# Attention and a capacity-routed mixture of experts: the planner knows when a load's room is free, and phase 1's routing starts two remainders later

## The chip, the core and the metric

The kernel runs on one core of a Trainium2 chip. Each core has five engines with their own instruction queues: TensorE (PE: matrix products, with a weight load ahead of each matmul, shown as PEld), VectorE (DVE), ScalarE (ACT), GpSimd (POOL) and SyncE (SP). ACT, DVE and POOL run their instructions in the order in which they are written. Transfers are issued from SP and POOL queues and carried out by 16 DMA engines that all queues share. The metric is the time of one execution in microseconds of the device.

## The reference

```python
def _attn_ref(q, k, v):                      # q, k, v: 8 x 8 x 576 x 64
    scores = scale * np.matmul(q, k.transpose(0, 1, 3, 2))
    mask = (rel >= 0) & (rel < window)       # window 64
    ...
    return np.matmul(attn, v)

def _moe_ref(x, w_gate, w1, w2):             # x: 4608 x 512, 8 experts
    logits = x @ w_gate
    order = np.argsort(-logits.flatten())
    for idx in order:
        tok, e = (int(idx) // E, int(idx) % E)
        if assigned[tok] >= 0 or counts[e] >= cap:      # cap = 576
            continue
        assigned[tok] = e
        counts[e] += 1
    for e in range(E):
        mask = assigned == e
        h = np.maximum(x[mask] @ w1[e], 0.0)            # 512 -> 1024
        out[mask] = h @ w2[e]                           # 1024 -> 512
```

Attention with a sliding window of 64 gives 4608 tokens of 512 values. The tokens are given to experts greedily, the highest logit first, 576 to each expert. Each token then goes through the two layers of its expert.

## The kernel before

The first part (`attention`) computes the attention for all tokens and stores them to a tensor in memory. The second part has eight phases, one for each expert. In phase p the routing (`Routing.steps(p)`) finds which expert fills up next, and which tokens it gets: it computes each free token's best choice on DVE (`choices`, lines 448 to 455), finds the threshold in eight rounds of comparing on DVE (line 463) and counting on TensorE (lines 522 and 536), and makes a list of the expert's 576 tokens. The rounds need each other's results, so the routing of a phase is one long chain of small steps; the routing of phase p + 1 begins where that of phase p ends.

From the routing of a phase two streams start. `Experts.load(p)` brings the expert's weights: eight chunks of 512 KB (four of w1, four of w2) go from memory to six staging buffers `st` (line 789, issued from SP, but from POOL for the last four of phase 0). ACT rounds a chunk to `wh` (line 810), writes its negative to `wl` (line 819), and an accumulating DMA from POOL adds `st` to it (line 821), so that `wh` and `wl` together are the full weight. The first three chunks of phase 0 take a subtraction on DVE in place of it (line 814). A ring of eight pairs `wh`, `wl` holds one expert's weights; a chunk of the next phase enters when one is given back (line 805). A staging buffer comes free when its add has landed; with six buffers, chunk i needs the buffer of the chunk six before it.

`Experts.turn(p)` gathers the tokens with five indirect DMAs from POOL (line 862), transposes them on TensorE (line 875, two PSUM buffers `tp`), rounds them to `xh` on ACT (line 852) and takes the remainder `xl` on DVE (line 856), in tiles of 128 tokens. `Experts.steps(p)` does the products: sixteen units of the first layer, each twelve matmuls of 128 rows of h by 256 or 320 tokens (line 921: `wh xh`, `wl xh`, `wh xl`), with three PSUM rooms `h`. A unit is read by ACT (`hh`, line 893) and then by DVE (`hl`, line 898), which frees its room. The second layer (lines 953 and 963) follows, with its results scattered to the output by indirect DMAs from POOL (line 943).

The order of all this on each engine is written out in advance by a planner (`Streams`): a small event clock in nanoseconds, in which every stream (routing, loads, gathers, products, evacuations) is a generator. A generator that yields a number goes on after that time; one that yields a function goes on when the function is true. An instruction is put on its engine's queue at the moment at which its generator reaches it. The planner's clock has prices for matmuls and rough ones for DVE, POOL and the DMAs; the engines then wait for the real data. So a wrong price never makes a wrong result, but an instruction may stand too early in an engine's queue and hold up what is behind it.

In `load`, `there[i]` is the time at which the planner takes chunk i to have landed. Before ACT's instruction for the chunk is put down, the planner waits for the ring, and then for that time:

```python
t = max(self.clock(), there.get(i - 1, 0)) + (LOAD if p else 1500) * (1 if i else 2)
...
yield lambda: self.taken - self.ring < self.used
if there[i] > self.clock():
    yield there[i] - self.clock()
```

The constants are LOAD = 2600 and ADDED = 4500. `self.lows[p]` counts the tiles of phase p whose remainder (line 856) has been put down.

Of the kernel before, what the change touches and what calls it, by code (L numbers as in the profile page):

```python
# [281 lines left out]
def consts(tc, cp):  # L282
    nc = tc.nc
    c = dict(pool=cp, zero=cp.tile([128, 128], BF, name="zero"))

    c["jp"] = cp.tile([128, 128], I32, name="jp")
    c["rel"] = cp.tile([128, 128], I32, name="rel")
    nc.gpsimd.iota(c["jp"], pattern=[[1, 128]], base=0, channel_multiplier=-1)
    return c
# [58 lines left out]
class Routing:  # L348


    def __init__(self, ctx, tc, c, V):
        self.tc, self.nc, self.c, self.V = tc, tc.nc, c, V
        nc = tc.nc
        rt = ctx.enter_context(tc.tile_pool(name="rt", bufs=1))
        self.rt, self.ctx = rt, ctx

        def t(name, shape, dt=FT):
            x = rt.tile(shape, dt, name=name)
            setattr(self, name, x)
            return x  # L360

        for name in ("eid", "un", "m", "best"):
            t(name, [128, NJ])
        for name in ("oh", "w", "one"):
            t(name, [128, NJ, E], BF)
        t("G0", [128, NJ, ND], BF)
        t("cw", [128, E])
        t("dg", [128, ND], I32)
        t("lane", [128, 1])
        t("rows", [128, 1], U32)  # L370
        self.setup = self.constants(c["jp"], t)
        self.idx, self.eint = {}, {}
# [364 lines left out]
NCH = 4  # L737
# [3 lines left out]
STAGE = 6  # L741
# [3 lines left out]
LOAD = 2600  # L745
ADDED = 4500
# [3 lines left out]
class Experts:  # L750
    def __init__(self, ctx, tc, c, xs, w1, w2, out, ring=8):
        self.tc, self.nc, self.c = tc, tc.nc, c
        self.xs, self.w1, self.w2, self.out = xs, w1, w2, out
        self.ring = ring
        self.fw = ctx.enter_context(tc.tile_pool(name="fw", bufs=1))
        self.ps = ctx.enter_context(tc.tile_pool(name="fp", bufs=1, space=PSUM))
        self.W = {}
        self.XT = {}
        self.used = 0
        self.taken = 0  # L760
        self.first = 0
        self.gathered = 0
        self.sent = 0
        self.turned = 0
        self.tiles = [0] * E
        self.lows = [0] * E
# [10 lines left out]
    def load(self, p, ei):  # L777

        nc, fw = self.nc, self.fw
        yield lambda: self.taken == 2 * NCH * p  # L780
        e = nc.sync.value_load(ei[0:1, 0:1], min_val=0, max_val=E - 1)
        eg = nc.gpsimd.value_load(ei[0:1, 0:1], min_val=0, max_val=E - 1) if p == 0 else None
        st, there = {}, {}

        def fetch(i):
            st[i] = fw.tile([128, 1024], FT, name="st", bufs=STAGE)

            q, r = (nc.gpsimd, eg) if p == 0 and i >= 4 else (nc.sync, e)
            q.dma_start(st[i], self.part(i, r))

            t = max(self.clock(), there.get(i - 1, 0)) + (LOAD if p else 1500) * (1 if i else 2)
            if p == 0 and i == 4:

                t = max(t, self.clock() + self.busy(0, "pool") + FIRST)
            there[i] = t

        ahead = 3 if p else 4
        for i in range(ahead):
            fetch(i)
        if p == 0:  # L800
            yield lambda: self.gathered
        for i in range(2 * NCH):
            if p == 0 and i == 3:
                yield lambda: self.tiles[0] > 1
# [3 lines that stand above are left out]
            hi = fw.tile([128, 1024], FR, name="wh", bufs=self.ring)  # L808
            lo = fw.tile([128, 1024], FR, name="wl", bufs=self.ring)
            nc.scalar.activation(hi, st[i], AF.Copy)  # L810
            yield 1050
            yield lambda: self.gathered > p
            if self.quick(p, i):
                nc.vector.tensor_tensor(lo, st[i], hi.bitcast(FT), OP.subtract)
                self.W[p, i] = (hi, lo)
                dt = self.busy(1130, "dve")
            else:

                nc.scalar.activation(lo, hi.bitcast(FT), AF.Copy, scale=-1.0)  # L819
                yield 1150  # L820
                nc.gpsimd.dma_start(lo.bitcast(FT), st[i], accum_op=OP.add)  # L821
                self.spawn(self.ready(p, i, hi, lo), self.busy(650, "pool") + ADDED - 1200)
                dt = 1300
            self.taken += 1
            if i + ahead < 2 * NCH:
                fetch(i + ahead)
            yield max(100, dt - 1200) if p or i < 3 else 900
# [178 lines left out]
def body(tc, q, k, v, vt, wg, w1, w2, xs, out):  # L1006
    nc = tc.nc
    with ExitStack() as ctx:
        cp = ctx.enter_context(tc.tile_pool(name="cp", bufs=1))
        ctx.enter_context(tc.manual_schedule())  # L1010
        c = consts(tc, cp)
        wgs = cp.tile([128, HP, 32], FT, name="wgs")
        L = cp.tile([128, NJ, E], FT, name="L")
        rt = Routing(ctx, tc, c, L)
        with ExitStack() as actx:
            attention(actx, tc, c, q, k, v, vt, (wgs, wg), xs, L, lambda j0, j1: rt.choices(j0, j1, 0), rt.setup,
                      rt.counters)
        rt.start()
        ex = Experts(ctx, tc, c, xs, w1, w2, out)
        rt.spare = ex.room  # L1020

        st = Streams()
        ex.spawn, ex.busy, rt.busy, ex.clock = st.add, st.busy, st.busy, lambda: st.now
        ex.warm, ex.rows, rt.prime = rt.warm, rt.rows, ex.prime

        def route():
            for p in range(E):
                for dt in rt.steps(p):
                    if p in rt.eint and p not in known:
                        known.add(p)  # L1030
                        st.add(ex.load(p, rt.eint[p]))
                    if p in rt.idx and p not in listed:
                        listed.add(p)
                        st.add(ex.turn(p, rt.idx[p]))
                    yield dt

        def products():
            for p in range(E):
                yield lambda: p in ex.XT
                yield from ex.steps(p, rt.idx[p])  # L1040

        known, listed = set(), set()
        st.add(route())
        st.add(products())
        st.run()
# [17 lines left out]
```

## Time and profile before

| | |
|---|---|
| median of three runs | 671.07 us (670.53 to 671.51) |
| the profiled execution | 669.82 us, span 668.1 us |
| mean granted TensorE clock | 0.980 |
| TensorE busy | 636.8 us, 95% of the span |
| VectorE, ScalarE, GpSimd busy | 443.7, 361.7, 186.5 us |
| moved by DMA | 134.10 MB, mean 201 GB/s |

The span runs from the first to the last instruction. Attention takes it up to about 165 us; then comes the routing of phase 0, in which TensorE has little to do, and from 200 us to the end the products of the eight phases. In the timeline's rows the first number is the start in microseconds from the span's start, the second the length; then come the engine, the line, the operation, and what is written from what. A number in square brackets is the idle time of the engine just before, and what ended it. A row with xN is N instructions in a row.

### The profile page before, as it was taken

Reading aid. Unit: us, or ns where it says so; the run is one execution under the profiler, and the core shown is the slowest. Engines: PE = TensorE matmul, PEld = TensorE weight load, DVE = VectorE, ACT = ScalarE, POOL = GpSimd, SP = SyncE. Lnnn points to the kernel's source line nnn. Section 1 sums busy time; section 2 is a strip of 40 time slices with the busy share of each in tenths; the row PEclk is TensorE's granted clock in tenths of the full one; section 3 lists DMA queues with packets and bytes.
Section 4 is the critical chain, followed back from the end, with each engine's and each line's share of the span. In section 5 each row is a group of like instructions: output and inputs, shape, how many; then the busy total and the mean of one; then the engine's idle time right before and its main releaser. Section 6 shows DMA issues by size and latency. Waiting matters only on the chain. (4 is left out here: it accounts for less than half of the span.)

```text
span 668.1 us, 16948 instructions
## 1 busy us (share of the span) xinstructions
PE 636.8 (95%) x6383; PEld 535.1 (80%) x6383; DVE 443.7 (66%) x2246; ACT 361.7 (54%) x733; POOL 186.5 (28%) x218
## 2 busy tenths in 40 slices
PE   8999999997479999999999999999999999999995
PEld 6667777776459878987997898799889879879984
DVE  5878898888787776875796787688578742221300
ACT  5788988885056156427626543662744366534310
POOL 0433233330061033206304231530512155212111
PEclk9999999999579999999999999999999999999999
DMA  9999988922069169729757956965987598983401
GB/s 301 352 374 373 368 321 313 380 74 81 3 216 233 33 241 241 164 87 273 194 97 267 221 123 181 246 165 100 289 196 154 184 226 249 231 230 83 91 25 47
DMA packets 50097, 134.10 MB, mean 201 GB/s; under 512 B 4696, under 2 KB 10968, under 8 KB 50016
## 3 DMA queue, kind: packets, MB, share of 16 engines
q0 software_dynamic: 15280, 52.98, 35.3%
q1 hardware_dynamic: 34192, 79.52, 33.5%
q8 instruction: 50, 0.82, 0.5%
q10 hardware_dynamic: 544, 0.52, 0.2%
q14 instruction: 31, 0.25, 0.1%
HBM read 82.15 MB, written 18.87 MB: 151 GB/s over the span
## 5 line engine op out<-in xcount | busy, mean ns | idle before, releaser
L943 POOL DMA_INDIRECT out<-ot,idx x40 | 41.9, 1047 | 271.0 <-DVE ot L941 79.2
L893 ACT ACTIVATE hh<-h 128x256 fp32r<-128x256 f32 (+1 forms) x128 | 52.0, 408 | 99.2 <-PE h L921 98.1
L898 DVE SCALAR_TENSOR_TENSOR hl<-h,hh 128x256 fp32r<-128x256 f32 x128 | 53.3, 417 | 77.0 <-ACT hh L893 76.1
L963 PE MATMUL o<-wh,hh 128*128 128x512 f32 x256 | 102.5, 401 | 0.0
L963 PE MATMUL o<-wl,hh 128*128 128x512 f32 x256 | 101.8, 398 | 0.0
L963 PE MATMUL o<-wh,hl 128*128 128x512 f32 x256 | 101.5, 396 | 0.0
L135 DVE CUSTOM_DVE_ANT_0 st<-Sp,mask 128x128 f32<-128x128 f32 x288 | 78.9, 278 | 21.4 <-PE Sp L126 15.1
L145 ACT ACTIVATE pe<-st,mx 128x128 f32<-128x128 f32 x288 | 91.2, 391 | 3.3 <-DVE mx L135 3.3
L921 PE MATMUL h<-xh,wl 128*128 128x256 f32 (+1 forms) x512 | 93.0, 299 | 0.0
L921 PE MATMUL h<-xl,wh 128*128 128x256 f32 (+1 forms) x512 | 92.1, 298 | 0.6 <-DVE xl L856 0.6
L921 PE MATMUL h<-xh,wh 128*128 128x256 f32 (+1 forms) x512 | 91.9, 299 | 0.7 <-ACT xh L852 0.7
L921 PEld LDWEIGHTS h<-xh,wh 128*128 128x128 f32 x512 | 75.9, 189 | 1.5 <-ACT xh L852 0.8
L921 PEld LDWEIGHTS h<-xl,wh 128*128 128x128 f32 x512 | 75.7, 190 | 0.9 <-DVE xl L856 0.9
L921 PEld LDWEIGHTS h<-xh,wl 128*128 128x128 f32 x512 | 76.1, 190 | 0.2
L810 ACT ACTIVATE wh<-st 128x1024 fp32r<-128x1024 f32 x64 | 67.2, 1050 | 10.4 <-DMA st<-w 10.4
L821 POOL DMA_DIRECT2D wl<-st x61 | 56.5, 1245 | 35.7 <-ACT wl L819 33.4
L819 ACT ACTIVATE wl<-wh 128x1024 fp32r<-128x1024 f32 x61 | 64.4, 1056 | 0.8
L935 ACT ACTIVATE ot<-o 128x512 f32<-128x512 f32 x32 | 19.1, 598 | 81.6 <-PE o L963 80.1
L963 PEld LDWEIGHTS o<-wh,hl 128*128 128x128 f32 x256 | 48.1, 188 | 9.4 <-issue 0.4
L963 PEld LDWEIGHTS o<-wh,hh 128*128 128x128 f32 x256 | 48.2, 188 | 8.9
L963 PEld LDWEIGHTS o<-wl,hh 128*128 128x128 f32 x256 | 48.2, 188 | 8.6
L862 POOL DMA_INDIRECT xg<-xs,idx x40 | 40.9, 1024 | 45.5 <-DVE eq L706 35.1
(177 smaller groups left out, 1134.9 us busy)
## 6 DMA issues: line engine op xcount, KB each, us to landing
wl<-st POOLq DMA_DIRECT2D x61, 512.0 KB, 8.2
st<-w SPq DMA_DIRECT2D x60, 512.0 KB, 7.5
xs<-x SPq DMA_DIRECT2D x36, 256.0 KB, 4.9
VO<-v SPq DMA_DIRECT2D x6, 1168.0 KB, 17.0
VT<-vt SPq DMA_DIRECT2D x6, 1152.0 KB, 11.5
Q<-q SPq DMA_DIRECT2D x6, 1152.0 KB, 14.2
K<-k SPq DMA_DIRECT2D x6, 1152.0 KB, 15.7
VO<-v SPq DMA_DIRECT2D x4, 584.0 KB, 11.3
```

The lines of the kernel that those rows point to most:

```text
L135: nc.vector.tensor_tensor_reduce(st[:, h, :], Sp[h % 2][:, h // 2], mk, scale=-0.125, scalar=3.0e38, op0=OP.add, op1=OP.min, accum_out=mx[ ...
L145: nc.scalar.activation(pe[:, h, :], st[:, h, :], AF.Exp, bias=mx[:, h:h + 1], scale=-1.0)
L810: nc.scalar.activation(hi, st[i], AF.Copy)
L819: nc.scalar.activation(lo, hi.bitcast(FT), AF.Copy, scale=-1.0)
L821: nc.gpsimd.dma_start(lo.bitcast(FT), st[i], accum_op=OP.add)
L862: nc.gpsimd.indirect_dma_start(out=g[0:n, a], out_offset=None, in_=self.xs, in_offset=IndirectOffsetOnAxis(ap=idx[0:n, a:a + 1], axis=0))
L893: nc.scalar.activation(hh[:, f, c0:c1], h, AF.Relu)
L898: nc.vector.scalar_tensor_tensor(t, h[:, a - c0:b - c0], 0.0, hh[:, f, a:b].bitcast(FT), op0=OP.max, op1=OP.subtract)
L921: nc.tensor.matmul(h, wv[:, cc, 128 * (f % 2):128 * (f % 2) + 128], xt[:, cc, c0:c1], start=(k == 0), stop=(k == 11))
L935: nc.scalar.activation(ot, o, AF.Copy)
L943: nc.gpsimd.indirect_dma_start(out=self.out, out_offset=IndirectOffsetOnAxis(ap=idx[0:m, a:a + 1], axis=0), in_=ot[0:m], in_offset=None)
L963: nc.tensor.matmul(o, ht[:, f, 128 * a:128 * a + 128], wt[:, 512 * (f % 2):512 * (f % 2) + 512], start=(k == 0), stop=(k == 23))
```

## The change

There are two edits. The first: when a chunk's add is put down, the planner notes the time at which it reckons the add to have landed, plus 1000, in a new table `added`, under the chunk's number counted over all phases. A load's `there` then counts from the latest of the clock, the load before, and the note of the chunk six before, whose staging buffer it takes. The second: the routing generator of phase 1 first yields a function that is true once the remainders of two tiles of phase 0 have been put down.

```diff
@@ class Experts, __init__
         self.W = {}
+        self.added = {}
@@ load, fetch(i)
-            t = max(self.clock(), there.get(i - 1, 0)) + (LOAD if p else 1500) * (1 if i else 2)
+
+            t = max(self.clock(), there.get(i - 1, 0), self.added.get(2 * NCH * p + i - STAGE, 0))
+            t += (LOAD if p else 1500) * (1 if i else 2)
@@ load
                 nc.gpsimd.dma_start(lo.bitcast(FT), st[i], accum_op=OP.add)
-                self.spawn(self.ready(p, i, hi, lo), self.busy(650, "pool") + ADDED - 1200)
+                t = self.busy(650, "pool") + ADDED - 1200
+                self.spawn(self.ready(p, i, hi, lo), t)
+                self.added[2 * NCH * p + i] = self.clock() + t + 1000
@@ route
             for p in range(E):
+                if p == 1:
+                    yield lambda: ex.lows[0] > 1
                 for dt in rt.steps(p):
```

No instruction of an engine is added or taken away; the edits act on the order in which the planner writes them.

## The prediction

> **What bounds the kernel now.** I read the page first, then TensorE's idle time by stretches, then who it waited for, then the timeline at each place where it waits.
>
> ```profile
> span 668.1 us, 16948 instructions
> ...
> L898 DVE SCALAR_TENSOR_TENSOR hl<-h,hh 128x256 fp32r<-128x256 f32 x128 | 53.3, 417 | 77.0 <-ACT hh L893 76.1
> ...
> 168.00:185.00 17.00, 7.78 (x225) 6.54 (x224) 12.52 (x68) 0.00 (x0) 1.07 (x1) 0.50 0.01 3
> 185.00:200.00 15.00, 11.22 (x97) 8.99 (x98) 12.51 (x31) 8.19 (x11) 9.60 (x10) 0.81 0.76 236
> 200.00:656.00 456.00, 453.27 (x3178) 399.11 (x3178) 279.52 (x1107) 219.50 (x345) 129.96 (x135) 1.00 0.69 177
> ...
> 584.00:596.00 12.00, 10.55 (x51) 8.34 (x52) 3.99 (x8) 5.20 (x9) 1.83 (x2) 1.00 1.05 284
> ```
>
> The first two lines are the page's (the group of DVE's remainders hl is used further down), the rest the busy times of stretches: the second number is the length, the third TensorE's busy time, and the last three are the granted clock, the DMA share and GB/s. TensorE (PE) bounds the kernel: from 200 to 656 us it is busy 453.27 of 456.00 us, so all products together wait only 2.73 us, and half of that lies at 584 to 596 (1.45 us). What an edit can win here is small; what it can lose is not bounded that way, since whatever makes TensorE wait is added to the end one for one. Waits from 185 us on:
>
> ```profile
> PE tp L875 <- DVE xl L856: 1.7, 2, 1.2
> ...
> PE h L921 <- DVE xl L856: 0.6, 1, 0.6
> ```
>
> The second edit aims at the last of these (0.6 us), the first at the first (1.7 us). I take them in that order.
>
> **The second edit, at its own place.** The new wait keeps phase 1's whole routing stream (six choices on DVE, then its counting rounds, loads and gathers) behind the remainders xl (L856) of phase 0's first two tiles.
>
> ```profile
> xg<-xs,idx POOLq DMA_INDIRECT x1, 4.9
> ...
> 192.59 2.00 POOL L862 DMA_INDIRECT xg<-xs,idx  x1 [0.30 <-issue]
> ...
> 194.09 1.22 DVE L814 TENSOR_TENSOR wl<-st,wh 128x1024 fp32r<-128x1024 f32 x1
> ...
> 195.23 0.45 DVE L448 TENSOR_REDUCE m<-L 128x36 f32<-128x288 f32 x1
> 195.27 0.60 ACT L852 ACTIVATE xh<-tp 128x512 fp32r<-128x512 f32 x1 [0.51 <-PE tp L875]
> 195.59 0.68 DVE L856 TENSOR_TENSOR xl<-tp,xh 128x512 fp32r<-128x512 f32 x1
> ...
> 197.05 0.68 DVE L856 TENSOR_TENSOR xl<-tp,xh 128x512 fp32r<-128x512 f32 x1
> ...
> 197.78 0.39 PE L921 MATMUL h<-xl,wh 128*128 128x256 f32 x1 [0.65 <-DVE xl L856]
> ...
> 198.01 0.46 PE L875 MATMUL tp<-identr,xg 128*128 128x128 f32 x4
> ```
>
> DVE works in order: L814, a choice, xl of tile 0, two choices, xl of tile 1, and TensorE sits until 197.78. Without the three choices the second xl needs only its xh (195.27 + 0.60 = 195.87), runs to about 196.6, and the gap of 0.65 us closes. But one matmul later TensorE transposes tile 2, whose gather was issued at 192.59 and takes 4.9 us: 197.5. It starts at 198.01 now, so only about 0.3 us can be kept. Gain 0.3 us (bounds 0 and 0.65).
>
> **What the second edit moves.** No instruction is added, but everything phase 1's routing issues comes later in the written order, and since TensorE is full and in order, a counting matmul (L536) that stands later in its queue runs later. How much: from the first choice's start to the end of the second xl is 197.73 - 195.23 = 2.5 us. At least 1.4 us (the second xl done at 196.6 instead of a choice at 195.23). At most about 4: then the six choices, 0.45 us each, also stand between the remainders of tiles 2 to 4 that they are ahead of now. I take 2.5 us. The routing has no wait at which it could catch up, and each phase's routing begins where the last one's ended, so I carry this lag through all phases. It moves SyncE's six loads of a phase, POOL's five gathers, and the POOL adds that make wl behind the gathers. Where that has room it costs nothing: the products of a phase are covered by the phase before. Where it has none:
>
> ```profile
> 238.38 3.40 SPq L789 DMA_DIRECT2D st<-w  x6
> ...
> 248.00:266.00 18.00, 18.00 (x124) 15.38 (x123) 11.71 (x41) 12.70 (x21) 8.57 (x9) 1.00 1.03 259
> ...
> 269.74 1.06 ACT L810 ACTIVATE wh<-st 128x1024 fp32r<-128x1024 f32 x1 [0.56 <-DMA st<-w]
> ...
> 270.70 0.42 ACT L893 ACTIVATE hh<-h 128x320 fp32r<-128x320 f32 x1
> ...
> 272.15 0.59 PE L536 MATMUL rps<-G,one 128*128 128x60 bf16 x9 [0.22 <-DVE G L463]
> ...
> 273.36 0.75 PE L921 MATMUL h<-xh,wh 128*128 128x320 f32 x4
> ...
> 328.39 1.06 ACT L810 ACTIVATE wh<-st 128x1024 fp32r<-128x1024 f32 x1 [0.31 <-DMA st<-w]
> ...
> 329.35 0.42 ACT L893 ACTIVATE hh<-h 128x320 fp32r<-128x320 f32 x1
> ...
> 331.99 0.75 PE L921 MATMUL h<-xh,wh 128*128 128x320 f32 x4
> ...
> 386.92 1.06 ACT L810 ACTIVATE wh<-st 128x1024 fp32r<-128x1024 f32 x1
> ```
>
> The loads of chunks 6 and 7 of a phase need the rooms of its chunks 0 and 1, which the adds free. Loads, gathers and adds run together at a DMA share of 1.03, so the train that starts 2.5 us late also ends 2.5 us late. ScalarE (ACT) reaches chunk 7 at 269.74 with 0.56 us of waiting already: the load lands just then. The lag makes this a wait of 3.06 us. Behind it on ACT stands hh of unit 4 (L893), and behind that on DVE its hl (0.42 us) and then a counting round's G. Unit 7 of the products (273.36) needs unit 4's PSUM room, of which there are three. Now the room is free at 270.70 + 0.42, and one and a half hl of 0.417 us later (256 and then 64 columns, the second one shorter): 271.75, 1.6 us early; so by the rooms TensorE loses 2.5 - 1.6 = 0.9 us. Through DVE's G, which TensorE already waits 0.22 us for, it could lose up to the whole 3.06 us. I take 1.3 us, near the lower end, as the row of the last phase (below) turns 5.4 us of ACT waiting into 1.7 us on TensorE. In phase 2 the same rows stand at 328.39 (0.31 us of waiting), 329.35 and 331.99: the room is 1.6 us early, so again 0.9 us by the rooms, at most 2.5 + 0.31 = 2.8 us, and again 1.3 us taken. In phase 3 ACT reaches chunk 7 at 386.92 without waiting, and by its issue and landing times:
>
> ```profile
> 375.69 0.33 SPq L789 DMA_DIRECT2D st<-w  x1
> ...
> st<-w SPq DMA_DIRECT2D x1, 512.0 KB, 8.7
> ```
>
> the load landed at 384.4. The 2.5 us before its use swallow the lag: 0, as in phases 4 to 6. If the lag is 4 us, it costs nothing there yet by the rooms, 1.5 us at the worst.
>
> **The last stall.** TensorE's largest loss stands at the end of phase 6:
>
> ```profile
> 556.62 1.05 ACT L819 ACTIVATE wl<-wh 128x1024 fp32r<-128x1024 f32 x1
> ...
> 557.43 1.02 POOL L943 DMA_INDIRECT out<-ot,idx  x1 [9.56 <-DVE hl L898]
> ...
> 565.07 1.01 POOL L943 DMA_INDIRECT out<-ot,idx  x1 [0.30 <-issue]
> 566.08 3.74 POOL L821 DMA_DIRECT2D wl<-st  x4
> ...
> 571.01 0.33 SPq L789 DMA_DIRECT2D st<-w  x1
> ...
> 575.54 0.38 ACT L893 ACTIVATE hh<-h 128x256 fp32r<-128x256 f32 x1
> 580.48 1.06 ACT L810 ACTIVATE wh<-st 128x1024 fp32r<-128x1024 f32 x1 [4.56 <-DMA st<-w]
> ...
> 582.54 1.02 ACT L893 ACTIVATE hh<-h 128x320 fp32r<-128x320 f32 x3
> ...
> 584.89 1.06 ACT L810 ACTIVATE wh<-st 128x1024 fp32r<-128x1024 f32 x1 [0.85 <-DMA st<-w]
> ...
> 585.00 0.53 PE L875 MATMUL tp<-identr,xg 128*128 128x128 f32 x4 [1.25 <-DVE xl L856]
> ...
> 587.21 0.54 PE L875 MATMUL tp<-identr,xg 128*128 128x128 f32 x4 [0.46 <-DVE xl L856]
> ```
>
> ACT stands 4.56 us at chunk 2 of phase 7 while three evacuations wait behind it (582.54, three in a row); the transposes wait for xl behind those, 1.25 + 0.46 = 1.71 us. The load could start only at 571.01, once the add of phase 6's chunk 4 (split by 557.67, issued at 566.08) had freed the room. That add stood on POOL behind an out (557.43), five gathers and another out, and the first out had waited 9.56 us, which I read as waiting for the out before it to land behind phase 6's first adds in POOL's queue. These adds follow the gathers, so they come the lag later, and this chain has no slack: 2.5 us more (bounds 1.4 and 4; 0 if the first out's wait has another cause).
>
> **The first edit.** It lets the planner set a chunk's earliest time to when the room is reckoned free, plus 2600. It adds no instruction; it can only place L810 later on ACT. By the code's constants an add is reckoned 650 on POOL, 4500 - 1200 and 1000 after its issue, so 4.95 us, plus what POOL has queued. For chunk 2 of phase 7, with all of POOL's 557.43 to 566.08 in front, that gives 557.67 + 8.4 + 4.95 = 571.0, plus 2.6 = 573.6 us. But the chunk stands behind the evacuation at 575.54 already, because the ring of eight must first give a room back. The reckoned time is never the last condition, so I cost this edit at 0: its cover is the ring's condition. In the other phases chunks 4 to 7 wait for the ring far longer, until the phase before has ended. If it did bind, the three evacuations would come first and the 1.71 us would be won.
>
> **The sum.** -0.3 + 1.3 + 1.3 + 2.5 = +4.8 us on the profiled execution's 669.82 us, 674.6. This execution lies 1.25 us under the median shown, 671.07, so I forecast 675.9 us against it. With a lag of 1.4 us and nothing lost by the rooms it is 671.8 (-0.65 + 1.4); with 4 us, 2.4 us each by the rooms and 4 in the last stall, 671.07 - 0.3 + 8.8 = 679.6.
>
> **Rivals.**
> 1. The lag is lost on the way (DMA makes it up in its idle stretches, or routing closes up on DVE) and only the gap at 197 remains: -0.3 us, 670.8. For it: the DMA share is 0.69 over the products. Against it: around 250 to 266 it is 1.03, and ACT waits already.
> 2. The first edit does bind at chunk 2 of phase 7 (the planner's clock for POOL may run ahead of what I reckoned by more than 2 us), the evacuations move ahead of L810 and the stall goes: 671.07 - 1.7 - 0.3 = 669.1, faster. It decides once the reckoned room is later than 575.54 - 2.6 = 572.9, where I get 571.0. A lag that puts the gathers later on POOL pushes that way; the ring's own condition speaks against it.
> 3. The clock drops as well. The first gap of the last stall would be 1.25 + 2.5 = 3.75 us in one piece. At 168 to 185 the granted clock is 0.50 with TensorE busy 7.78 of 17 us, and the return takes until 200 (0.81 over 15 us, so 5.7 us at half speed, a loss of 2.85 us). The same after the stall: 678.8. In the present gap the clock stays 1.00, so I hold it unlikely. [...]
> 4. The wait changes nothing, because two remainders are out when phase 0's routing ends: 671.1. Against it: L448 at 195.23 stands before both.
>
> **How the numbers follow.** The lag as worked out 0.60 (own range 671.8 to 679.6), the clock too 0.05, lag lost 0.16, first edit binds 0.15, no change 0.04. Two runs of this kernel can be told apart from about 0.2%, 1.3 us. Faster by more than that is rival 2 (0.15) and little of rival 1 (0.02): 0.17. Slower is 0.65 less the low edge of the first case (0.03): 0.62. The same is the rest, 0.21. The range goes from 669.9, which takes in rivals 1 and 4, to 679.6.
>
> **What would show it.** The choices (L448) start behind the second xl and the gap of 0.65 us before the xl products is under 0.4: step one. Phase 1's six loads start later than 238.38 by 1.4 to 4 us: the lag. ACT's L810 waits for st near 268 and 328 by 2 to 3 us each, and TensorE's idle time from 200 to 656 rises from 2.73 to about 8 us, with the last stall at 4 us: the losses. If the loads start 2 us later and ACT's waits do not grow, the carrying through DMA is wrong; if the 4.56 us wait is gone and three evacuations stand before that L810, the first edit binds and I am wrong in sign.

## Result: the changed kernel is slower, by more than was forecast

| | before | after |
|---|---|---|
| median of five runs | 670.67 us (669.60 to 671.51) | 683.75 us (679.32 to 684.70) |
| ratio, with its 95% interval | | 1.018 (1.0162 to 1.0197) |
| the profiled execution | 669.82 us, span 668.1 | 679.32 us, span 677.7 |

The profiled execution of the changed kernel is the shortest of its five; the others are some 4 us longer. Two profiles of longer executions with the same lag stand under the first experiments.

The products fall into eight phases, and the first matmul of a phase's first layer bounds each. The two fences give the busy times of these stretches, first of before (phases 0, 1, 2, then 2 to 5 together, and 6), then of after. After the bounds come the length, the busy times of TensorE (with its matmuls), of the weight load, VectorE, ScalarE and GpSimd; the last three numbers are the granted clock, the DMA share and GB/s.

```profile
195.92:260.76 64.84, 64.19 (x454) 53.98 (x455) 46.10 (x177) 32.58 (x50) 20.84 (x24) 1.00 0.68 181
260.76:319.67 58.91, 58.56 (x426) 51.41 (x425) 44.19 (x180) 29.43 (x46) 16.75 (x18) 1.00 0.72 184
319.67:378.64 58.97, 58.79 (x436) 51.62 (x434) 44.01 (x181) 29.69 (x46) 17.40 (x18) 1.00 0.74 189
...
319.67:554.71 235.04, 234.36 (x1720) 206.43 (x1719) 172.59 (x704) 117.04 (x182) 70.68 (x72) 1.00 0.73 190
554.71:610.07 55.36, 53.66 (x325) 48.09 (x324) 11.31 (x30) 26.90 (x42) 17.94 (x19) 1.00 0.77 207
```

```profile
196.06:258.91 62.85, 62.79 (x438) 52.97 (x438) 42.49 (x162) 31.19 (x48) 20.01 (x24) 1.00 0.62 174
258.91:325.36 66.45, 61.81 (x445) 53.83 (x444) 45.97 (x184) 30.83 (x49) 17.62 (x19) 0.97 0.67 172
325.36:384.65 59.29, 58.45 (x427) 51.38 (x426) 43.96 (x179) 29.66 (x47) 17.61 (x18) 1.00 0.72 184
...
325.36:562.19 236.83, 235.14 (x1721) 206.56 (x1719) 175.45 (x715) 118.00 (x183) 68.84 (x71) 1.00 0.72 186
562.19:619.61 57.42, 53.94 (x326) 48.16 (x324) 11.12 (x30) 26.68 (x42) 17.95 (x19) 1.00 0.78 214
```

The span grew by 9.60 us, and the lengths say where: the products begin 0.14 later; phase 0 is 1.99 shorter, phase 1 is 7.54 longer; phases 2 to 5 are 1.79 longer, phase 6 is 2.06 longer, and phase 7, from the last bound to the span's end, 0.06 (58.09 against 58.03). Phase 0 lost 16 matmuls (454 to 438) and phase 1 won 19: counting matmuls of the late routing moved across the bound. So phases 0 and 1 belong together: +5.55 us, of which TensorE stands idle for 3.70 more (4.70 against 1.00, length less busy) and is busy for 1.85 more. The clock of 0.97 in phase 1 says that the busier part is slower matmuls. Of the 1.99 us by which phase 0 is shorter, 0.59 are idle time (0.65 to 0.06 us) and the rest is work that moved.

**The gap at 197 us** is gone. Timeline of after:

```profile
195.24 1.50 DVE L861 TENSOR_TENSOR xl<-tp,xh 128x512 fp32r<-128x512 f32 x2
...
196.65 0.44 DVE L448 TENSOR_REDUCE m<-L 128x36 f32<-128x288 f32 x1
...
197.25 0.45 PE L880 MATMUL tp<-identr,xg 128*128 128x128 f32 x4
```

The two remainders run in one piece, the first choice comes behind them, and the next tile's transposes start at 197.25 where they started at 198.01.

**Phase 1.** The loads and gathers are later, and the products earlier. Loads of after, from SP's queue:

```profile
240.85 3.86 SPq L790 DMA_DIRECT2D st<-w  x6
...
260.10 0.33 SPq L790 DMA_DIRECT2D st<-w  x1
```

The load of chunk 6 before (two loads in one row), and ACT at that chunk:

```profile
256.86 3.44 SPq L789 DMA_DIRECT2D st<-w  x2
...
266.86 1.05 ACT L810 ACTIVATE wh<-st 128x1024 fp32r<-128x1024 f32 x1
267.80 0.43 ACT L893 ACTIVATE hh<-h 128x320 fp32r<-128x320 f32 x1
```

The six loads start 2.47 us later (238.38 to 240.85), and the load of chunk 6, which needs a room that an add behind the late gathers frees, 3.24 (256.86 to 260.10). The products of phase 1 start 1.85 us earlier (260.76 to 258.91). From the first load to the first product were 22.38 us and are 18.06: seen from the products the lag is 4.3 us, and 5.1 at chunk 6. Timeline of after in phase 1, by ACT, DVE and TensorE:

```profile
270.32 1.06 ACT L813 ACTIVATE wh<-st 128x1024 fp32r<-128x1024 f32 x1 [4.62 <-DMA st<-w]
...
272.37 0.42 ACT L898 ACTIVATE hh<-h 128x320 fp32r<-128x320 f32 x1
...
272.82 0.42 DVE L903 SCALAR_TENSOR_TENSOR hl<-h,hh 128x256 fp32r<-128x256 f32 x1 [5.05 <-ACT hh L898]
...
273.52 0.59 PE L926 MATMUL h<-xh,wh 128*128 128x256 f32 x3 [2.77 <-DVE ps L561]
...
274.73 0.31 PE L536 MATMUL rps<-G,one 128*128 128x60 bf16 x5 [0.61 <-DVE G L463]
...
276.10 0.36 PE L536 MATMUL rps<-G,one 128*128 128x60 bf16 x4 [1.06 <-DVE G L463]
...
276.64 1.05 PE L926 MATMUL h<-xh,wl 128*128 128x256 f32 x4
```

ACT reaches chunk 6 at 265.70 (270.32 - 4.62) and stands there, where it went straight in at 266.86 before. Behind it, and behind the chunk's negative (L822), waits an hh (267.80 before, 272.37 now), behind that on DVE an hl, and behind that the routing's small steps and G. TensorE waits for the room (the profile names ps, the DVE instruction right behind the hl's) and then twice for G: 2.77 + 0.61 + 1.06 = 4.44 of ACT's 4.62 us. The last row is four matmuls in 1.05 us, against 0.64 at full clock (the same form in phase 0, 196.65). Stretches of after, of two microseconds:

```profile
274.00:276.00 2.00, 0.43 (x7) 0.23 (x6) 1.46 (x6) 1.47 (x3) 0.87 (x1) 0.93 1.11 219
276.00:278.00 2.00, 1.90 (x12) 1.90 (x12) 1.83 (x11) 0.00 (x0) 0.00 (x0) 0.50 1.02 203
278.00:280.00 2.00, 2.00 (x12) 2.00 (x12) 1.41 (x7) 0.38 (x1) 0.00 (x0) 0.72 1.11 219
```

The granted clock falls to one half: from the three stretches, 2 x 2 us x (0.07 + 0.50 + 0.28) = 3.4 us at half clock, a loss of 1.7 us of products. A clock of 0.93 over the first of them puts the fall 0.28 us before its end, at 275.7.

**The last stall.** Timeline of after, with ACT, TensorE and SP's load of chunk 2; the first two rows belong to a wait of their own:

```profile
576.85 0.99 ACT L898 ACTIVATE hh<-h 128x256 fp32r<-128x256 f32 x3 [3.83 <-PE h L926]
...
577.75 0.42 PE L926 MATMUL h<-xh,wh 128*128 128x320 f32 x1 [1.17 <-DVE hl L903]
...
580.41 0.33 SPq L790 DMA_DIRECT2D st<-w  x1
...
589.64 1.06 ACT L813 ACTIVATE wh<-st 128x1024 fp32r<-128x1024 f32 x1 [4.81 <-DMA st<-w]
594.15 0.53 PE L880 MATMUL tp<-identr,xg 128*128 128x128 f32 x4 [1.50 <-DVE xl L861]
...
596.73 0.54 PE L880 MATMUL tp<-identr,xg 128*128 128x128 f32 x4 [0.81 <-DVE xl L861]
```

ACT waits at chunk 2 of phase 7 for 4.81 us (4.56 before) and TensorE behind it for 2.31 (1.71). In this execution phase 6 was held up by 1.17 us ahead of that, so ACT came to the chunk later, too, and the lag shows little there. In other executions it shows more (next section).

### The profile page after: what moved, and what is told of

Its sections match the earlier page's. It is cut to its first block, busy times and chain, and to the rows that moved or that the text cites. A ratio compares the mean times of both kernels' runs of the same rounds, so it can differ in the third digit from the quotient of the medians.

```text
span 677.7 us, 16952 instructions
## 1 busy us (share of the span) xinstructions
PE 638.8 (94%) x6383; PEld 536.3 (79%) x6383; DVE 444.7 (66%) x2246; ACT 362.4 (53%) x733; POOL 184.9 (27%) x218
## 5 line engine op out<-in xcount | busy, mean ns | idle before, releaser
L926 PE MATMUL h<-xh,wh 128*128 128x256 f32 (+1 forms) x512 | 93.4, 301 | 4.6 <-DVE ps L561 2.8
L822 ACT ACTIVATE wl<-wh 128x1024 fp32r<-128x1024 f32 x61 | 64.4, 1056 | 0.9
L173 PE MATMUL Op<-VO,pt 128*64 128x73 f32 x640 | 52.4, 233 | 0.4 <-DVE x L198 0.3
```

Of the source, the lines that this page charges most:

```text
L173: nc.tensor.matmul(Op[64 * a:64 * a + 64, h, :], pt[:, h, 64 * a:64 * a + 64], vv[a][:, 4 * g + h, :], start=True, stop=True)
L926: nc.tensor.matmul(h, wv[:, cc, 128 * (f % 2):128 * (f % 2) + 128], xt[:, cc, c0:c1], start=(k == 0), stop=(k == 11))
```

## The experiments

**Which edit.** One kernel with the first edit alone (the generator's new wait taken out of the changed kernel), one with the second alone:

```diff
# e1_first_edit: the changed kernel without the second edit
-                if p == 1:
-                    yield lambda: ex.lows[0] > 1
# e2_second_edit: the kernel before with the second edit
+                if p == 1:
+                    yield lambda: ex.lows[0] > 1
```

> The first edit alone. Its instructions stand in the same order on every engine as those of the kernel before. Theory (the table of rooms is never the last condition): no change, 671.1 us within 0.2%. Rival: any clear difference.

> The second edit alone, without the table of rooms. Theory (the lag of phase 1's routing does all of it, the table nothing): the time of the changed kernel, 679 to 685 us, with ACT's long wait at chunk 6 of phase 1 (about 4.6 us). Rival (the table moves chunks on ACT and costs part of it): clearly under 679 us.

First edit: 670.92 us, ratio 0.9998 (0.9987 to 1.001); engine by engine its instructions stand in the same order as before's. Second edit: 684.27 us, ratio 1.0195 (1.0174 to 1.0215), and its instructions stand in the changed kernel's order. The whole loss is the second edit's, and the first one never binds. Since this is the changed kernel's program once more, its profile also shows what a longer execution has. ACT and TensorE at the last stall:

```profile
594.06 1.06 ACT L810 ACTIVATE wh<-st 128x1024 fp32r<-128x1024 f32 x1 [8.82 <-DMA st<-w]
...
598.57 0.75 PE L875 MATMUL tp<-identr,xg 128*128 128x128 f32 x4 [5.51 <-DVE xl L856]
```

Stretches of it, behind each of the two stalls and phase 6 as a whole:

```profile
564.02:625.59 61.57, 56.06 (x325) 50.00 (x324) 11.39 (x30) 26.90 (x42) 17.94 (x19) 0.94 0.74 199
...
274.00:276.00 2.00, 1.22 (x8) 0.96 (x9) 1.56 (x7) 1.97 (x3) 0.66 (x1) 0.50 1.08 213
...
600.00:602.00 2.00, 2.00 (x9) 1.51 (x8) 0.81 (x2) 1.21 (x3) 0.87 (x1) 0.50 1.07 322
```

Here the wait ahead of the last stall is missing, ACT stands 8.82 us and TensorE 5.51 in one piece, and the clock falls to half twice, behind either stall. Phase 6 is 6.21 us longer than before (61.57 against 55.36): 3.81 of idle time and 2.40 of slower matmuls. The kernel with the lag alone, which comes next, was profiled at 684.69 us, and its phase 6 is nearly as long:

```profile
564.51:624.97 60.46, 55.27 (x326) 49.56 (x324) 11.38 (x30) 26.88 (x42) 17.93 (x19) 0.94 0.74 202
```

The changed kernel's other four executions have no profile of their own. That phase 6 makes them longer, too, is likely and not shown. The mean clock of an execution does not settle it: it is 0.967 to 0.973 in these four and 0.975 in the profiled one, but an execution of the lag alone took 683.21 us at 0.976.

**The place of the choices, or the lag.** The second edit does two things: it moves the choices behind the remainders, and all that follows in the routing comes later. The first kernel keeps both edits and gives the six choices less time in the planner, so that the routing catches up; the second leaves the choices where they were and puts a pause of 2440 ns behind them; the third waits for one remainder in place of two.

```diff
# e4_no_lag: the changed kernel, and in the choices' loop
-                    yield self.dve(490)
+                    yield 180 if p == 1 else self.dve(490)
# e5_lag_alone: the kernel before, and behind the choices' loop
+            if p == 1:
+                yield 2440
# e3_one_remainder: the changed kernel
-                    yield lambda: ex.lows[0] > 1
+                    yield lambda: ex.lows[0] > 0
```

> Both edits, but the planner reckons 180 for each of phase 1's choices in place of 490 and more, so that the counting rounds, loads and gathers are written where they were before; the six choices stay behind the two remainders. Theory (lag): loads of phase 1 at 238.4 again, ACT's wait there 0.6 us again, the gap of 0.65 us at 197 stays closed: 670.0 to 670.7 us. Rival (place of the choices): as slow as the changed kernel, over 677 us.

> The kernel before, with a wait of 2440 in the planner behind phase 1's six choices: the choices stay ahead of the remainders as before, and all that follows them has the lag. Theory (lag): 680 to 685 us, loads of phase 1 at about 241, ACT's wait of 4 to 5 us at chunk 6 of phase 1, and the gap of 0.65 us at 197 is there again. Rival (place of the choices): about 671 us.

> Both edits, but the routing of phase 1 waits for one tile's remainder in place of two. Theory (the loss follows the lag): phase 1's loads start about 1 us later than before in place of 2.5, ACT's wait at chunk 6 or 7 of phase 1 grows from 0.6 to 1 to 2 us, TensorE loses 0 to 2 us: 670 to 673 us. Rival (the loss comes from having the choices among the remainders of tiles 2 to 4 on DVE, whatever the lag): well over 673 us, since five of the six choices still stand there.

Without the lag: 670.62 us, 0.9994 (0.9984 to 1.0004). The lag alone: 684.92, 1.0211 (1.0178 to 1.0243). One remainder: 672.04, 1.0013 (1.0002 to 1.0024). So the choices' new place costs nothing and wins nothing that can be measured, and the lag is the whole loss. Without the lag ACT waits 0.56 us at chunk 7 of phase 1, as before. The gap at 197 us is closed there, but 3 us later TensorE waits for the third tile's remainder, which stands on DVE behind the choices and the first comparisons of the counting rounds:

```profile
201.78 0.49 PE L880 MATMUL tp<-identr,xg 64*128 64x64 f32 x4 [0.53 <-DVE xl L861]
```

The wait has moved; in the changed kernel's own profile it is absent. ACT at chunk 6 of phase 1 with the lag alone, then the loads and the same chunk with one remainder:

```profile
272.25 1.06 ACT L812 ACTIVATE wh<-st 128x1024 fp32r<-128x1024 f32 x1 [4.67 <-DMA st<-w]
```

```profile
239.23 4.01 SPq L790 DMA_DIRECT2D st<-w  x6
...
267.32 1.06 ACT L813 ACTIVATE wh<-st 128x1024 fp32r<-128x1024 f32 x1 [0.23 <-DMA st<-w]
```

and its phase 1:

```profile
260.89:320.79 59.90, 58.62 (x427) 51.41 (x425) 43.99 (x180) 29.81 (x47) 17.38 (x18) 1.00 0.73 185
```

With one remainder the first load leads the products by 21.66 us (260.89 - 239.23), a lag of 0.7 where two remainders give 4.3; phases 0 and 1 together are 0.5 us longer than before (64.33 + 59.90 against 123.75) and the clock stays full. By these two points the loss is not in proportion to the lag: a small lag is mostly paid from margins, and a large one is paid nearly whole, with the clock on top.

**Where the lag is paid.** If ACT's standing at a late chunk with evacuations behind it is the cause, then placing the chunk later on ACT, behind those evacuations, must win the time back while the transfers stay late. Two kernels do this to the changed kernel, for chunk 6 of phase 1 and for this and chunk 2 of phase 7:

```diff
             if there[i] > self.clock():
                 yield there[i] - self.clock()
+            if (p, i) in LATER:
+                yield LATER[p, i]
# e6_later16:    LATER = {(1, 6): 6000}
# e9_later_both: LATER = {(1, 6): 6000, (7, 2): 9000}
```

> The changed kernel, with ACT's instruction for chunk 6 of phase 1 (and so chunk 7 behind it) written 6 us later in the planner's clock, behind the evacuations that stood waiting behind it; loads and adds stay as late as they are. Theory (the late load costs only because ACT stands in front of the evacuations): TensorE's idle time in phase 1 goes, its clock stays at 1.00 there, and some 6 us of the loss with it: 676 to 679 us. Rival (the products or the counting rounds themselves come too late for want of weights): still over 682 us, the wait moved to another row.

> The changed kernel, with both of ACT's instructions written later: chunk 6 of phase 1 by 6 us and chunk 2 of phase 7 by 9 us. Theory: both big losses go, and what is left over the time before is the 2 us of phases 2 to 5, less the 1.7 us that the kernel before lost in the last stall and the 0.7 us of the gap: 669 to 672 us. Rival (the lag costs elsewhere too): over 675 us.

The first: 675.86 us, ratio 1.0074 (1.0047 to 1.0101). Both: 671.70, 1.0009 (0.9993 to 1.0025). Phase 1 of the first and its load of chunk 6; then phases 2 to 5, and 6, of the second:

```profile
260.03:320.03 60.00, 59.87 (x444) 52.41 (x444) 45.58 (x184) 30.67 (x49) 17.76 (x19) 1.00 0.74 191
...
261.13 0.33 SPq L791 DMA_DIRECT2D st<-w  x1
```

```profile
320.33:557.24 236.91, 235.00 (x1721) 206.48 (x1720) 175.43 (x715) 118.04 (x183) 68.78 (x71) 1.00 0.72 186
557.24:611.22 53.98, 53.43 (x325) 48.25 (x324) 11.56 (x30) 26.95 (x42) 18.05 (x19) 1.00 0.84 226
```

In phase 1 TensorE's idle time falls from 4.64 to 0.13 us, in phase 6 from 3.48 to 0.55, although the loads are as late as in the changed kernel: the one of chunk 6 starts 1.10 us behind the first product of phase 1 (261.13 - 260.03), there 1.19 (260.10 - 258.91). By the medians the stand at chunk 6 costs 7.9 us (683.75 - 675.86) and the one at chunk 2 of phase 7 costs 4.2 (675.86 - 671.70); by the ratios to the kernel before, 7.1 and 4.4 us. The bandwidth of DMA was not the price; the order on ACT was. Phases 2 to 5 keep 236.91 us here (235.04 before), so the lag costs between one and two microseconds there, in small waits.

**The clock.** Twenty-six small matmuls, whose results nothing reads, go ahead of unit 6 of phase 1 in the changed kernel, to fill the first of its waits:

```diff
# e8_dummies
+            if p == 1 and n == 6:
+                x = self.ps.tile([128, DM], FT, name="o", bufs=2)[:, 0:288]
+                for _ in range(26):
+                    nc.tensor.matmul(x, self.ones, self.r32[:, 0:8], start=True, stop=True)
```

> The changed kernel, with 26 matmuls whose result nobody uses (about 0.12 us each) ahead of unit 6 of phase 1, where TensorE stands idle. Theory (part of phase 1's loss is the clock at half speed after the idle time): the clock stays at 1.00 behind the stall, the stall itself stays, and 1.5 to 3 us are won: 680 to 682 us. Rival (the clock costs nothing that the stall does not): no gain or up to 1 us lost.

682.44 us, ratio 1.0171 (1.0145 to 1.0197). Phase 1 of it:

```profile
260.21:325.26 65.05, 63.40 (x471) 54.95 (x470) 45.70 (x184) 30.79 (x49) 17.15 (x19) 1.00 0.68 176
```

ACT still waits at chunk 6, the clock stays at 1.00, and the phase is 1.40 us shorter than the changed kernel's (66.45) and 1.58 shorter than with the second edit alone (66.63). With phase 0 it is 1.49 us (127.81 against 129.30). That is about what a spell of 3.4 us at half clock costs, 1.7 us. In the total the gain of 1.3 to 1.8 us lies inside the intervals, and this profile shows one reason: the clock falls in phase 6 instead (0.97 over the phase, in which TensorE waits 2.9 us in one piece at the transposes), and phase 6 takes 59.37 us against the changed kernel's 57.42. So the price of the clock is shown for phase 1, and not for the whole time.

**The last stall by itself.** Three kernels: the kernel before with chunk 2 of phase 7 placed 9000 ns later; the kernel before with a lag of 3600 ns in phase 6's routing alone; and the lag of 2440 ns in phase 1, with phase 2's choices cut to 60 ns in the planner, so that the routing catches up after phase 1.

```diff
# e7_later72:   LATER = {(7, 2): 9000}, in the kernel before
# e10_lag_at_6: the kernel before, behind the choices' loop
+            if p == 6:
+                yield 3600
# e11_lag_in_1: the lag alone, and in the choices' loop
-                    yield self.dve(490)
+                    yield 60 if p == 2 else self.dve(490)
```

> The kernel before, with ACT's instruction for chunk 2 of phase 7 written 9 us later. Theory: the wait of 4.56 us on ACT stands behind the evacuations and the transposes' roundings, TensorE's 1.71 us at 584 to 588 goes: 669.0 to 669.6 us. Rival (the transposes are held by their own remainders on DVE): no change.

> The kernel before with a wait in the planner in phase 6's routing alone, behind its choices, which writes the gathers of phases 6 and 7 some 1.8 us later; phases 1 to 5 are as before. Theory (a lag of the gathers lengthens the last stall by way of POOL's queue): loss in the last stall alone, ACT's wait at chunk 2 of phase 7 from 4.6 to 6.5 us or more, 673 to 676 us. Rival (the last stall grew in the changed kernel only because of what went before): 671 us.

> The kernel before with the wait of 2440 in phase 1's routing, and phase 2's choices reckoned at 60 each, so that from phase 2 on gathers are written where they were before. Theory (each phase's lag costs for itself): the loss of phase 1 alone, 5.5 to 7 us, 677 to 678 us, the last stall as before. Rival (the loss of phase 1 is only shifted and comes back or grows later): over 681 us.

Later chunk: 670.25 us, ratio 0.998 (0.9969 to 0.9991). Lag in phase 6: 673.29, 1.0033 (1.0019 to 1.0046). Lag in phase 1 alone: 675.06, 1.0048 (1.003 to 1.0065). The later chunk takes the transposes' wait away, but less is won than the 1.71 us of it, and less than was expected: in the profile another wait stands in phase 6, 1.1 us of TensorE for ACT, which starts three evacuations at 568.44 after 2.38 us of idling (the last section has more on this wait).

Timeline with the lag in phase 6:

```profile
569.92 0.99 ACT L895 ACTIVATE hh<-h 128x256 fp32r<-128x256 f32 x3 [4.38 <-PE h L923]
...
568.57 3.74 POOL L823 DMA_DIRECT2D wl<-st  x4
...
573.52 0.33 SPq L791 DMA_DIRECT2D st<-w  x1
...
582.77 1.06 ACT L812 ACTIVATE wh<-st 128x1024 fp32r<-128x1024 f32 x1 [4.87 <-DMA st<-w]
```

POOL's four adds behind the gathers come 2.49 us later (566.08 to 568.57), and the load of chunk 2 goes out 2.51 us later (571.01 to 573.52): the routing's lag does reach this load through POOL's queue, as the prediction had it. ACT's wait grew only by 0.31, because it came to the chunk behind evacuations that were late themselves (569.92), at 577.90 and not at 575.92. How much of a lag shows at this stall thus depends on whether that other wait appears. In phase 1 alone the lag gave a smaller loss than with it in all phases, and a smaller one than expected. Phases 2 to 5 and phase 6:

```profile
325.95:561.41 235.46, 234.33 (x1721) 206.43 (x1719) 172.67 (x704) 117.12 (x182) 70.51 (x72) 1.00 0.73 190
561.41:617.23 55.82, 53.90 (x325) 48.09 (x324) 11.12 (x30) 26.82 (x42) 17.94 (x19) 1.00 0.76 206
```

Phases 2 to 5 and phase 6 are nearly as long as before (235.04 and 55.36): their losses come from a lag that is carried on, and go when it is caught up. But this kernel is no clean cut. ACT waits 3.26 us, up to 254.86, for the last of phase 2's choices, which the planner takes to be done sooner; the roundings `xh` of phase 1 stand behind it, and the products start only at 262.72 us. So the lag against the products, and ACT's wait at chunk 6 (2.72 us), are smaller than with two remainders, while phases 0 and 1 together are 5.21 us longer than before (65.73 + 63.23) in the profiled execution, the slowest of five. What the lag costs in phase 1 by itself is therefore read from the kernels with later chunks, not from this one.

**A version that beats both.** The later chunk 2 of phase 7 on top of the kernel with both edits and no lag:

```diff
# e12_no_lag_later72: e4_no_lag with LATER = {(7, 2): 9000}
```

> Choices behind the two remainders without the lag, and ACT's chunk 2 of phase 7 written 9 us later: what the two edits were after, by other means. Theory: the gap (0.6 us) and most of the last stall (0.9 us as measured alone) add up: 669.3 to 669.9 us against 671.1, faster than both kernels. Rival (the two do not add, since the stall moves to the products of phase 6): 670.3 us or more.

670.08 us, ratio 0.9979 (0.9967 to 0.9991): 0.2% faster than before, and not to be told from the later chunk alone (0.998). The gain is the chunk's place; the choices' place adds nothing that these runs can show. The profile fits: here, too, the wait for the third tile's remainder stands in place of the gap, with 0.73 us at 202.58.

## Why the prediction was right in sign and too small

- **The gap at 197 us: right, and under-sized.** It closed; the term was -0.3, the transposes came 0.76 us earlier, and TensorE idled 0.59 us less in phase 0. The step that failed is the gather of tile 2 taken as landing 4.9 us after its issue, at 197.5: after the change the transposes that need it run at 197.25 with no wait for it.
- **The lag: right as a time, wrong as a measure.** Phase 1's loads came 2.47 us later, against 2.5 taken. But the step "the lag makes this a wait of 3.06 us" held the products still. The routing that moved back left room in TensorE's queue, the gap was closed as well, and the products of phase 1 started 1.85 us earlier. What counts is the lag against the products: 4.3 us at the loads, 5.1 at chunk 6. So the wait came one chunk sooner than predicted, and was 4.62 us.
- **Phase 1's term: +1.3 taken, and this is the step that failed most; with the clock, which the sum had at nothing, it put the time outside the range.** Phases 0 and 1 together gave +5.55 in the profiled execution, and ACT's stand there is worth 7.1 to 7.9 us by the kernel with the later chunk. I chose near the lower end, by the rooms and by the last phase's row, in which 4.56 + 0.85 us of ACT's waiting cost TensorE 1.71; the range's upper edge, too, had phase 1 by the rooms alone. TensorE lost 4.44 of ACT's 4.62 us: 2.77 to the room and 1.67 to G. So the upper end, "the whole 3.06 us", was the one to take. That the last phase's row is so much cheaper because no routing stands on DVE behind it (DVE is busy for 11.31 us in phase 6, 44.19 in phase 1) is my reading; no run takes the routing out of phase 1. With the rest of the sum unchanged, the measured 4.4 us would have given 675.9 + 4.4 - 1.3 = 679.0, just inside the range; the clock's 1.7 us in phase 1 takes it to 680.7, outside.
- **The clock (rival 3, chance 0.05): it happened.** It came with the broken wait in phase 1 and, in the profiles of longer executions, with the last stall as well. The stall of 3.75 us in one piece, from which it was priced, was 5.51 us where it came there. The spells at half clock were 3.4 us long in the changed kernel's profile and twice 6.8 in that of the second edit alone. The latter are worked out as above, 2 x 2 us x (0.07 + 0.50 + 0.50 + 0.50 + 0.14) from 272 to 282 us and 2 x 2 us x (0.50 + 0.50 + 0.50 + 0.20) from 598 to 606. It was wrong to go by the length of one unbroken gap, as the last section shows.
- **Phase 2: +1.3 taken, too much.** ACT waited 1.22 us at its chunk 6, and the phase is 0.32 us longer (58.97 to 59.29). **Phases 3 to 5: 0 taken.** Phases 2 to 5 together gave +1.79, of which executions of before's own order differ by 0.8 (235.88 us with the first edit alone).
- **The last stall: +2.5 taken.** +2.06 in the profiled execution, +6.21 in that of the second edit alone; 4.2 to 4.4 by the kernels with later chunks. The way the lag takes through POOL is as predicted: the load of chunk 2 moved by 2.51 us when phase 6 alone was lagged. What was missed is the clock, and that the load itself took longer (582.81 to 594.06 us with the second edit alone, 9.5 us before).
- **The first edit: 0, right**, by the run with it alone. The rivals that the lag is lost and that the wait changes nothing are refuted by the phases' lengths.

## What to carry to other kernels

Price a delay against the work that needs the data, and not against the clock on the wall: what moves back out of an engine's queue lets the rest of that queue go ahead, and the two add up (here 2.47 and 1.85 us, 4.3 together). When an engine in written order must wait for a transfer, ask what stands behind it in its queue; placing the waiting instruction behind that work won the time back here, 7.1 to 7.9 us at one chunk and 4.2 to 4.4 at the other, with the transfers as late as they were. And when a change lets TensorE wait for some microseconds, add the price of the clock's fall to the wait, and do not go by the longest gap alone: here the clock fell behind waits of 2.77 and 2.81 us, and in the first case the spell of 3.4 us at half cost 1.7 us.

## What was not expected of the hardware

The clock fell behind gaps shorter than the 3.75 us from which rival 3 was priced. In the run of the second edit alone TensorE's last matmul before the stall ended at 271.74, and the clock was at half from about 273.7, 2 us later. A stretch of one microsecond, and the next matmuls:

```profile
273.00:274.00 1.00, 0.00 (x0) 0.00 (x0) 0.15 (x1) 1.00 (x3) 0.21 (x1) 0.86 1.00 201
...
274.55 0.98 PE L921 MATMUL h<-xh,wh 128*128 128x256 f32 x3 [2.81 <-DVE ps L561]
```

A clock of 0.86 over one microsecond is 0.28 us at half. In the changed kernel's profile the fall came at about 275.7, after 2.77 us of idling and 0.91 us of scattered work. So neither fall came behind a gap of 3.75 us, and the second came after work had begun again.

Nor did every stall bring a fall. Stretches of the changed kernel's profile, each as long as the spell at half: ahead of the fall, the spell, and in the last stall:

```profile
272.31:275.72 3.41, 0.91 (x8) 0.64 (x9) 2.25 (x10) 3.13 (x6) 1.47 (x2) 1.00 1.07 211
275.72:279.14 3.42, 3.04 (x16) 3.04 (x16) 2.73 (x15) 0.38 (x1) 0.26 (x1) 0.50 1.07 211
...
593.16:596.57 3.41, 1.76 (x9) 1.20 (x9) 1.53 (x4) 2.21 (x4) 0.00 (x0) 1.00 1.06 278
```

The waits of 1.50 and 0.81 us in the last stall left TensorE busy for 1.76 of 3.41 us, and the clock stayed at 1.00; ahead of the fall it was busy for 0.91 of 3.41, and ahead of the first fall with the second edit alone for 1.44 (270.31 to 273.72). The way back differed, too. In the changed kernel's profile the clock was at 1.00 again behind the 3.42 us of the second row, of which TensorE was busy for 3.04. With the second edit alone TensorE was busy for 2.27 of the 4.00 us from 274 to 278, and the clock stayed at half until about 280.6. What decides when it falls and when it returns no run here shows.

ACT can stand with its work ready. In the changed kernel three evacuations begin at 576.85 after 3.83 us of idling, for which the profile names TensorE; but the first of them reads a unit whose last matmuls ran from 572.74 for 0.64 us, so it was ready at 573.4. Such a stand, 13 to 15 us into phase 6, is in nine of the fourteen profiles, among them the one with the first edit alone, which has before's order (1.88 us), the one with the later chunk of phase 7 alone (2.38), and the one with the lag in phase 6 (4.38). It is missing in five: before, the second edit alone, which has the changed kernel's order, the lag alone, no lag, and one remainder. TensorE lost 1.1 to 1.7 us to it, and 0.5 us with both later chunks. What holds ACT there no view shows, and it stays open; it is one reason why the last stall's numbers scatter: of the kernels with the lag in all phases and ACT's chunks where the changed kernel has them, the two without this stand have the long phase 6 (61.57 and 60.46 us), the two with it 57.42 and 59.37.
